# Decode attention with a GeGLU gate: one stream of 2 MB cache loads with 16 KB rows in place of 256 KB loads with 2 KB rows

## The chip, the cores and the metric

The kernel runs on one core of one Trainium2 chip. The metric is device microseconds of one execution. Before the change it takes 151.41 us (median of 4 runs, 151.3 to 152.01). A run counts as slow when it is over 1.5% above the fastest of the same kernel; a single run of a kernel has no known state. The span of a profile is about 1.9 us shorter than the time, because it runs from the first to the last instruction. In the views, PE is the matrix engine, DVE and ACT are the vector and scalar engines, SP is the engine whose queue issues the loads, and SBUF is the on-chip memory that the loads fill, 128 partitions of it here. A packet is one record of the DMA trace; for these loads it is one row.

## The reference, cut to what matters

```python
xn = layernorm(x)                                  # x: 8 x 1 x 512
q  = (xn @ wq)                                     # 32 query heads of 128
k, v = k_cache[:, :, 3072:, :], v_cache[...]       # 8 batches, 8 kv heads, last 1024 of 4096 tokens
s  = softmax(q k^T / sqrt(128)) v @ wo             # 4 query heads share a kv head
g  = silu((gelu(xn @ w_gate) * (xn @ w_up)) @ w_down)
out = x + s * g
```

The window of one (batch, kv head) pair is 256 KB without a gap; the next head's window begins 1 MB further on. All inputs are bf16: 33.6 MB of K and V windows (8 batches, K and V, 2 MB each) and 13.9 MB of weights, 47.5 MB together. The loads set the floor: at the 416 GB/s of the weight stretch below, 47.5 MB would take 114 us (an estimate from that stretch) of the 149.5.

## The kernel before

```python
    for hkv in range(Hkv):                       # K stage
        for b in range(B):
            k_sb = k_pool.tile([P, NSC, Dh], BF16, name="k_sb")          # 6 buffers
            nc.sync.dma_start(out=k_sb,
                in_=A_k_cache[b, hkv, win0:Sk, :].rearrange("(p c) d -> p c d", c=NSC))
            ...8 transposes -> kT_ps; copy to kT; 8 score matmuls, 4 wide; exp -> pT_all
    ...softmax sums for all pairs                # [cut]
    for hkv in range(Hkv):                       # V stage
        for b in range(B):
            ...load v_sb the same way; 8 value matmuls; oT_all = oT_ps * 1/sum
        nc.sync.dma_start(out=wo_sb[:, hkv*rep:(hkv+1)*rep, :], in_=...)   # 1 KB rows
        ...4 matmuls of 512 columns into s_ps
```

One load is one head's window: 128 partitions, 8 tokens each, so 128 rows of 2 KB. Source and destination both have one outer dimension of 128. wq, the FFN weights and the FFN come first, then all of K, then all of V with wo in eight pieces.

The softmax here doesn't subtract the row's maximum and nothing guards it: scores larger than these inputs give would overflow.

Of the kernel before, what the change touches and what calls it, by code (L numbers as in the profile page):

```python
# [7 lines left out]
ACT = mybir.ActivationFunctionType  # L9
# [3 lines left out]
FP32 = mybir.dt.float32  # L13


@with_exitstack
def kernel(
# [22 lines left out]
    NDC = D // 128  # L40
    NFC = F // 128
    NSC = W // 128
    inv_sqrt_dh = float(Dh) ** -0.5

    P = nc.NUM_PARTITIONS
    NG = Hkv * B
    GB = 16

    consts = ctx.enter_context(tc.tile_pool(name="consts", bufs=1))
    weights = ctx.enter_context(tc.tile_pool(name="weights", bufs=1))  # L50
    persist = ctx.enter_context(tc.tile_pool(name="persist", bufs=1))
    ffn_sb = ctx.enter_context(tc.tile_pool(name="ffn_sb", bufs=1))
    k_pool = ctx.enter_context(tc.tile_pool(name="k_pool", bufs=6))
    kT_pool = ctx.enter_context(tc.tile_pool(name="kT_pool", bufs=4))
    v_pool = ctx.enter_context(tc.tile_pool(name="v_pool", bufs=20))
    small = ctx.enter_context(tc.tile_pool(name="small", bufs=3))
# [4 lines left out]
        out=ident,  # L61
        in_=ident,
        compare_op=ALU.not_equal,
        fill=1.0,
        base=0,
        pattern=[[-1, P]],
        channel_multiplier=1,
    )
    ones_pp = consts.tile([P, P], BF16, name="ones_pp")
    nc.vector.memset(ones_pp, 1.0)  # L70

    x_flat = A_x.flatten_outer_dims()
    x_sb = persist.tile([B, D], BF16, name="x_sb")
    nc.sync.dma_start(out=x_sb, in_=x_flat)

    wq_sb = weights.tile([P, NDC, Hq * Dh], BF16, name="wq_sb")
    nc.sync.dma_start(out=wq_sb, in_=A_wq.rearrange("(k p) n -> p k n", p=P))
    wg_sb = weights.tile([P, NDC, F], BF16, name="wg_sb")
    nc.scalar.dma_start(out=wg_sb, in_=B_w_gate.rearrange("(k p) n -> p k n", p=P))
    wu_sb = weights.tile([P, NDC, F], BF16, name="wu_sb")  # L80
    nc.gpsimd.dma_start(out=wu_sb, in_=B_w_up.rearrange("(k p) n -> p k n", p=P))
    wd_sb = weights.tile([P, NFC, D], BF16, name="wd_sb")
    nc.scalar.dma_start(out=wd_sb, in_=B_w_down.rearrange("(k p) n -> p k n", p=P))
    wo_sb = weights.tile([P, Hq, D], BF16, name="wo_sb")

    eps_sb = consts.tile([B, 1], FP32, name="eps_sb")
    nc.vector.memset(eps_sb, 1e-5)

    stats = persist.tile([B, nc.vector.BN_STATS_DIM], FP32, name="stats")
    nc.vector.bn_stats(out=stats, in_=x_sb)  # L90
    mv = persist.tile([B, nc.vector.BN_AGGR_DIM], FP32, name="mv")
    nc.vector.bn_aggr(out=mv, in_=stats)
    rstd = persist.tile([B, 1], FP32, name="rstd")
    nc.scalar.activation(
        out=rstd, in_=mv[:, 1:2], func=ACT.Sqrt, bias=eps_sb, scale=1.0
    )
    nc.vector.reciprocal(out=rstd, in_=rstd)
    xhat = persist.tile([B, D], BF16, name="xhat")
    nc.vector.tensor_scalar(  # L99
        out=xhat,  # L100
        in0=x_sb,
        scalar1=mv[:, 0:1],
        scalar2=rstd[:, 0:1],
        op0=ALU.subtract,
        op1=ALU.mult,
    )

    xnT_sb = persist.tile([P, NDC, B], BF16, name="xnT_sb")
    qT_all = persist.tile([P, B, Hq], BF16, name="qT_all")
    oT_all = persist.tile([P, Hq, B], BF16, name="oT_all")  # L110
    hT_sb = persist.tile([P, NFC, B], BF16, name="hT_sb")
    g_sb = persist.tile([B, D], FP32, name="g_sb")
    pT_all = persist.tile([P, NG, NSC, rep], BF16, name="pT_all")
    sums_sb = persist.tile([P, NG, rep], FP32, name="sums_sb")
    recip_all = persist.tile([P, NG, rep], FP32, name="recip_all")

    with tc.tile_pool(name="ps_xnT", bufs=1, space=bass.MemoryType.PSUM) as ps_xnT_pool:
        xnT_ps = ps_xnT_pool.tile([P, NDC, B], BF16, name="xnT_ps")
        for k in range(NDC):
            nc.tensor.transpose(  # L120
                xnT_ps[:, k, :],
                xhat[:, k * 128 : (k + 1) * 128],
                ident[0:B, 0:B],
            )
        nc.vector.tensor_copy(out=xnT_sb, in_=xnT_ps)

    HB = 8
    qctx = ExitStack()
    ps_q = qctx.enter_context(tc.tile_pool(name="ps_q", bufs=2, space=bass.MemoryType.PSUM))
    for m0 in range(0, Hq, HB):  # L130
        qT_ps = ps_q.tile([P, HB, B], FP32, name="qT_ps")
        for mi in range(HB):
            m = m0 + mi
            for k in range(NDC):
                nc.tensor.matmul(  # L135
                    qT_ps[:, mi, :],
                    wq_sb[:, k, m * Dh : (m + 1) * Dh],
                    xnT_sb[:, k, :],
                    start=(k == 0),
                    stop=(k == NDC - 1),  # L140
                )
        nc.vector.tensor_copy(  # L142
            out=qT_all[:, :, m0 : m0 + HB],
            in_=qT_ps.rearrange("p h b -> p b h"),
        )

    fctx = ExitStack()
    ffn_ps = fctx.enter_context(tc.tile_pool(name="ffn_ps", bufs=1, space=bass.MemoryType.PSUM))
    gu_ps = ffn_ps.tile([P, NFC, 2, B], FP32, name="gu_ps")
    for j in range(NFC):  # L150
        for w, wsb in enumerate((wg_sb, wu_sb)):
            for k in range(NDC):
                nc.tensor.matmul(  # L153
                    gu_ps[:, j, w, :],
                    wsb[:, k, j * 128 : (j + 1) * 128],
                    xnT_sb[:, k, :],
                    start=(k == 0),
                    stop=(k == NDC - 1),
                )
    zT = gu_ps[:, :, 0, :]  # L160
    uT = gu_ps[:, :, 1, :]
    z2 = ffn_sb.tile([P, NFC, B], FP32, name="z2")
# [4 lines left out]
    u3 = ffn_sb.tile([P, NFC, B], FP32, name="u3")  # L167
    nc.vector.tensor_tensor(out=u3, in0=z2, in1=zT, op=ALU.mult)
    th = ffn_sb.tile([P, NFC, B], FP32, name="th")
    nc.scalar.activation(out=th, in_=u3, func=ACT.Tanh, scale=0.7978845608028654)  # L170
    gm = ffn_sb.tile([P, NFC, B], FP32, name="gm")
    nc.vector.tensor_scalar(
        out=gm, in0=th, scalar1=0.5, scalar2=0.5, op0=ALU.mult, op1=ALU.add
    )
    gz = ffn_sb.tile([P, NFC, B], FP32, name="gz")
    nc.vector.tensor_tensor(out=gz, in0=gm, in1=zT, op=ALU.mult)
    nc.vector.tensor_tensor(out=hT_sb, in0=gz, in1=uT, op=ALU.mult)

    f_ps = ffn_ps.tile([B, D], FP32, name="f_ps")
    for j in range(NFC):  # L180
        nc.tensor.matmul(  # L181
            f_ps,
            hT_sb[:, j, :],
            wd_sb[:, j, :],
            start=(j == 0),
            stop=(j == NFC - 1),
        )
    th2 = ffn_sb.tile([B, D], FP32, name="th2")
    nc.scalar.activation(out=th2, in_=f_ps, func=ACT.Tanh, scale=0.5)
    nc.vector.tensor_scalar(  # L190
# [4 lines left out]
    p1ctx = ExitStack()  # L195
    ps_kT = p1ctx.enter_context(tc.tile_pool(name="ps_kT", bufs=2, space=bass.MemoryType.PSUM))
    ps_sc = p1ctx.enter_context(tc.tile_pool(name="ps_sc", bufs=2, space=bass.MemoryType.PSUM))

    gi = 0
    for hkv in range(Hkv):  # L200
        for b in range(B):
            k_sb = k_pool.tile([P, NSC, Dh], BF16, name="k_sb")
            nc.sync.dma_start(
                out=k_sb,
                in_=A_k_cache[b, hkv, win0:Sk, :].rearrange(
                    "(p c) d -> p c d", c=NSC
                ),
            )
            kT_ps = ps_kT.tile([P, W], BF16, name="kT_ps")
            for c in range(NSC):  # L210
                nc.tensor.transpose(  # L211
                    kT_ps[:, c * 128 : (c + 1) * 128],
                    k_sb[:, c, :],
                    ident,
                )
            kT = kT_pool.tile([P, W], BF16, name="kT")
            nc.vector.tensor_copy(out=kT, in_=kT_ps)  # L217
            sc_ps = ps_sc.tile([P, NSC, rep], FP32, name="sc_ps")
            qg = qT_all[:, b, hkv * rep : (hkv + 1) * rep]
            for c in range(NSC):  # L220
                nc.tensor.matmul(  # L221
                    sc_ps[:, c, :],
                    kT[:, c * 128 : (c + 1) * 128],
                    qg,
                    start=True,
                    stop=True,
                )
            nc.scalar.activation(  # L228
                out=pT_all[:, gi, :, :],
                in_=sc_ps,  # L230
                func=ACT.Exp,
                scale=inv_sqrt_dh,
            )
            gi += 1
# [108 lines left out]
```

## Time and profile before

| | before |
|---|---|
| time | 151.4 us |
| span of the profile | 149.5 us |
| bytes moved, mean rate | 47.74 MB, 319 GB/s |
| wq and FFN weights, 4 to 22 us | 416 GB/s |
| K stage, 40 to 86 us | 304 GB/s, PE busy 40.3 of 46 us |
| V stage with wo, 88 to 142 us | 365 GB/s |

From the page of the kernel before, part 2: the span in 40 slices, in tenths; DMA is the busy share of the 16 DMA engines, GB/s what they moved.

```profile
PEclk9999999999999999689999999755555555555555
DMA  4999999957999699889989899999999999999900
GB/s 117 430 419 416 407 403 372 372 161 212 315 390 368 211 342 325 252 278 298 298 321 323 263 311 309 393 372 378 372 380 371 376 357 380 337 386 380 349 30 2
DMA packets 25843, 47.74 MB, mean 319 GB/s; under 512 B 2256, under 2 KB 8160, under 8 KB 25312
```

From the view by stretches of the kernel before; the last three columns are granted TensorE clock, DMA share and GB/s.

```profile
4.00:22.00 18.00, 2.16 (x63) 1.90 (x63) 0.53 (x2) 0.00 (x0) 0.00 (x0) 1.00 1.02 416
40.00:86.00 46.00, 40.27 (x817) 35.04 (x815) 36.94 (x56) 10.18 (x52) 0.00 (x0) 0.96 0.90 304
88.00:142.00 54.00, 35.70 (x605) 22.17 (x602) 16.31 (x69) 1.14 (x6) 0.00 (x0) 0.57 1.03 365
```

The chain of waits of the kernel before, part 4 of the page:

```profile
DMA 66%; PE 24%; DVE 5%; issue 3%; SPq 1%
```

Two lines of the view of what its load queue waited for (us in total, times, longest):

```profile
SPq L203 <- PE sc_ps L221: 21.0, 31, 1.0
...
SPq L203 <- PE kT_ps L211: 7.7, 19, 1.3
```

Read together: in the K stage the DMA engines are not always busy (0.90) and the queue waits for PE to give K buffers back. In the V stage they are always busy (1.03), yet move 365 GB/s where the weight stretch moved 416. So there are two things to win: PE work spread over more traffic, and longer rows.

### The profile page before, as it was taken

What the parts mean: (1) busy time and instruction counts of PE and PEld (TensorE: products, weight loads), DVE (VectorE), ACT (ScalarE), POOL (GpSimd) and SP (SyncE); (2) the same over time, 40 slices, a digit from 0 to 9 for tenths busy, and PEclk for the clock granted to TensorE, in tenths of its full rate; (3) what the DMA queues carried; (4) which work ended last, traced back from release to release, by engine and by line L of the source; (5) the groups of instructions that cost most, each with busy time, mean ns of one, the idle gap of its engine ahead of it and who ended that gap; (6) DMA issues with size and microseconds to landing.
All of it is one profiled execution on the core that took longest, in us unless ns stands there. A gap on an engine that the chain in (4) does not pass through costs nothing.

```text
span 149.5 us, 4236 instructions
## 1 busy us (share of the span) xinstructions
PE 97.0 (65%) x1830; PEld 73.4 (49%) x1830; DVE 64.2 (43%) x154; ACT 16.5 (11%) x70; POOL 1.4 (1%) x6
## 2 busy tenths in 40 slices
PE   0000137499988896998998996597474748585760
PEld 0000127497466785987876874453433334342420
DVE  2100001057296885788788885831211121121213
ACT  4000000052122221222222221000000000000000
POOL 3000000000000000000000000000000000000000
PEclk9999999999999999689999999755555555555555
DMA  4999999957999699889989899999999999999900
GB/s 117 430 419 416 407 403 372 372 161 212 315 390 368 211 342 325 252 278 298 298 321 323 263 311 309 393 372 378 372 380 371 376 357 380 337 386 380 349 30 2
DMA packets 25843, 47.74 MB, mean 319 GB/s; under 512 B 2256, under 2 KB 8160, under 8 KB 25312
## 3 DMA queue, kind: packets, MB, share of 16 engines
q1 hardware_dynamic: 23216, 41.97, 79.9%
q10 hardware_dynamic: 2336, 3.67, 7.1%
q0 software_dynamic: 272, 1.84, 2.9%
q8 instruction: 14, 0.23, 0.6%
q14 instruction: 5, 0.04, 0.1%
HBM read 47.46 MB, written 0.01 MB: 318 GB/s over the span
## 4 chain that ended last, share of the span: by engine, by line
DMA 66%; PE 24%; DVE 5%; issue 3%; SPq 1%
DMA v_sb<-in_A_v_cache_dram 22%; DMA k_sb<-in_A_k_cache_dram 17%; DMA wq_sb<-in_A_wq_dram 15%; DMA wo_sb<-in_A_wo_dram 12%; PE kT_ps L211 10%; PE s_ps L300 4%; PE sc_ps L221 4%; DVE kT L217 3%; PE qT_ps L135 2%; PE f_ps L181 2%; PE gu_ps L153 1%; SPq L269 1%; DVE tmp L309 0%; DVE out_sb L311 0%; SPq L292 0%
## 5 line engine op out<-in xcount | busy, mean ns | idle before, releaser
L217 DVE COPY kT<-kT_ps 128x1024 bf16<-128x1024 bf16 x64 | 43.6, 690 | 14.4 <-PE kT_ps L211 14.1
L211 PE MATMUL kT_ps<-ident,k_sb 128*128 128x128 bf16 x512 | 41.6, 228 | 3.2 <-DMA k_sb<-in_A_k_cache_dram 3.2
L211 PEld LDWEIGHTS <-k_sb 128*128 128x128 bf16 x512 | 31.3, 102 | 3.8 <-DMA k_sb<-in_A_k_cache_dram 3.8
L284 DVE TENSOR_TENSOR oT_all<-oT_ps,recip_all 128x4 bf16<-128x4 f32 x64 | 11.0, 175 | 36.4 <-PE oT_ps L277 35.4
L277 PE MATMUL oT_ps<-pT_all,v_sb 128*128 128x4 bf16 x512 | 19.9, 167 | 10.2 <-DMA v_sb<-in_A_v_cache_dram 7.3
L277 PEld LDWEIGHTS <-v_sb 128*128 128x128 bf16 x512 | 16.8, 105 | 19.4 <-DMA v_sb<-in_A_v_cache_dram 10.6
L221 PE MATMUL sc_ps<-qT_all,kT 128*128 128x4 bf16 x512 | 22.7, 166 | 3.8 <-DVE kT L217 1.7
L221 PEld LDWEIGHTS <-kT 128*128 128x128 bf16 x512 | 17.9, 97 | 10.0 <-DVE kT L217 8.5
L300 PE MATMUL s_ps<-wo_sb,oT_all 128*8 128x512 bf16 x32 | 14.9, 620 | 8.0 <-DMA wo_sb<-in_A_wo_dram 8.0
L228 ACT ACTIVATE pT_all<-sc_ps 128x32 bf16<-128x32 f32 x64 | 12.6, 197 | 43.9 <-PE sc_ps L221 43.9
L153 PE MATMUL gu_ps<-xnT_sb,wg_sb 128*128 128x8 bf16 x56 | 3.4, 168 | 12.5 <-DMA wg_sb<-in_B_w_gate_dram 10.4
L142 DVE CAST qT_all<-qT_ps 128x64 bf16<-128x64 f32 x4 | 0.9, 225 | 21.3 <-PE qT_ps L135 21.3
L300 PEld LDWEIGHTS <-oT_all 128*8 128x8 bf16 x32 | 3.3, 106 | 12.8 <-issue 10.3
L153 PEld LDWEIGHTS <-wg_sb 128*128 128x128 bf16 x56 | 2.7, 104 | 10.5 <-DMA wg_sb<-in_B_w_gate_dram 10.5
L135 PE MATMUL qT_ps<-xnT_sb,wq_sb 128*128 128x8 bf16 x128 | 3.6, 168 | 3.4 <-DMA wq_sb<-in_A_wq_dram 3.4
L135 PEld LDWEIGHTS <-wq_sb 128*128 128x128 bf16 x128 | 3.5, 104 | 3.5 <-DMA wq_sb<-in_A_wq_dram 3.5
L153 PEld LDWEIGHTS <-wu_sb 128*128 128x128 bf16 x56 | 2.6, 104 | 5.2 <-DMA wu_sb<-in_B_w_up_dram 3.0
L153 PE MATMUL gu_ps<-xnT_sb,wu_sb 128*128 128x8 bf16 x56 | 3.1, 168 | 2.9 <-DMA wu_sb<-in_B_w_up_dram 2.9
L163 ACT ACTIVATE z_381<-gu_ps 128x112 f32<-128x112 f32 x1 | 0.3, 264 | 26.8 <-PE gu_ps L153 26.8
L252 DVE TENSOR_REDUCE sums_sb<-sums_ps 128x64 f32<-128x512 f32 x4 | 2.7, 684 | 1.1 <-PE sums_ps L243 1.1
L181 PE MATMUL f_ps<-wd_sb,hT_sb 128*8 128x512 bf16 x14 | 3.2, 379 | 0.0
L120 PE MATMUL xnT_ps<-ident,xhat 8*128 8x8 bf16 x4 | 0.3, 168 | 4.4 <-DVE xhat L99 4.4
(33 smaller groups left out, 15.9 us busy)
## 6 DMA issues: line engine op xcount, KB each, us to landing
k_sb<-in_A_k_cache_dram SPq DMA_DIRECT2D x64, 256.0 KB, 4.3
v_sb<-in_A_v_cache_dram SPq DMA_DIRECT2D x64, 256.0 KB, 6.1
wq_sb<-in_A_wq_dram SPq DMA_DIRECT2D x1, 4096.0 KB, 22.0
wo_sb<-in_A_wo_dram SPq DMA_DIRECT2D x8, 512.0 KB, 6.2
wg_sb<-in_B_w_gate_dram ACTq DMA_DIRECT2D x1, 1792.0 KB, 14.3
wd_sb<-in_B_w_down_dram ACTq DMA_DIRECT2D x1, 1792.0 KB, 32.1
wu_sb<-in_B_w_up_dram POOLq DMA_DIRECT2D x1, 1792.0 KB, 16.9
x_sb<-in_A_x_dram SPq DMA_DIRECT2D x1, 8.0 KB
```

The source lines that it names most:

```text
L135: nc.tensor.matmul(qT_ps[:, mi, :], wq_sb[:, k, m * Dh : (m + 1) * Dh], xnT_sb[:, k, :], start=(k == 0), stop=(k == NDC - 1),)
L153: nc.tensor.matmul(gu_ps[:, j, w, :], wsb[:, k, j * 128 : (j + 1) * 128], xnT_sb[:, k, :], start=(k == 0), stop=(k == NDC - 1),)
L181: nc.tensor.matmul(f_ps, hT_sb[:, j, :], wd_sb[:, j, :], start=(j == 0), stop=(j == NFC - 1),)
L211: nc.tensor.transpose(kT_ps[:, c * 128 : (c + 1) * 128], k_sb[:, c, :], ident,)
L217: nc.vector.tensor_copy(out=kT, in_=kT_ps)
L221: nc.tensor.matmul(sc_ps[:, c, :], kT[:, c * 128 : (c + 1) * 128], qg, start=True, stop=True,)
L228: nc.scalar.activation(out=pT_all[:, gi, :, :], in_=sc_ps, func=ACT.Exp, scale=inv_sqrt_dh,)
L252: nc.vector.tensor_reduce(out=sums_sb[:, i * GB : (i + 1) * GB, :], in_=sums_ps.rearrange("p (g c j) -> p g j c", g=GB, c=NSC, j=rep), axi ...
L269: nc.sync.dma_start(out=v_sb, in_=A_v_cache[b, hkv, win0:Sk, :].rearrange("(p c) d -> p c d", c=NSC),)
L277: nc.tensor.matmul(oT_ps, v_sb[:, c, :], pT_all[:, gi, c, :], start=(c == 0), stop=(c == NSC - 1),)
L284: nc.vector.tensor_tensor(out=oT_all[:, hkv * rep : (hkv + 1) * rep, b], in0=oT_ps, in1=recip_all[:, gi, :], op=ALU.mult,)
L300: nc.tensor.matmul(s_ps, oT_all[:, h, :], wo_sb[:, h, :], start=(h == 0), stop=(h == Hq - 1),)
```

## The change

Its intent is one unbroken stream of large loads. A ring of ten 16 KB-per-partition slots takes all big loads in order. A slot holds a whole batch of K or V: eight heads, each on 16 partitions of 64 tokens, so a row is 16 KB. A chunk of 128 partitions then mixes eight heads, so scores are computed 32 wide for all query heads and a mask, added by a matmul with the identity, removes the wrong heads before the exponential. K and V of consecutive batches alternate; weights of the FFN and wo come last; the attention output is rearranged on chip to match 16 KB rows of wo.

```diff
-            nc.sync.dma_start(out=k_sb, in_=A_k_cache[b, hkv, win0:Sk, :].rearrange("(p c) d -> p c d", c=NSC))
+    def load_cache(cache, b, name):
+        t = ring.tile([P, NCH, Dh], BF16, name=name, tag="slot")        # ring: 10 slots
+        nc.sync.dma_start(
+            out=t.rearrange("p c d -> p (c d)"),
+            in_=cache[b, :, win0:Sk, :].rearrange("n (p c) d -> p n (c d)", p=PS),   # PS = 16
+        )
+    def load_rows(src, rows, r0, n, name): ...   # weights: [128, 16 KB] from "(p r) n -> p r n"
+    def scores(b, g):
+        nc.tensor.matmul(sc_ps, ident, mask, start=True, stop=False)     # 512 wide, new
+        for c in range(GC): nc.tensor.matmul(sc_ps[:, c, :], kT chunk, qT[:, b, :], ...)   # 32 wide
+    def values(b): ...4 sum matmuls of 512, 64 value matmuls 32 wide
+    for b in range(B):
+        k_t[b] = load_cache(A_k_cache, b, "k_t"); v_t[b-1] = load_cache(A_v_cache, b-1, "v_t")
+        ...transposes(b), scores(b), values(b-1) interleaved, in emission order
+    ...w_gate, w_up, last V, w_down, wo (last piece: 4 rows); FFN; output rows matched on chip
```

The destination of a cache load is 128 partitions. Its source is 16 token slices (16 KB apart) by 8 heads (1 MB apart), and it is given in that order.

## The prediction

> **What bounds the kernel now.** The execution moves 47.74 MB in a 149.5 us span (mean 319 GB/s, queue table); no engine is busy more than 65% of it. Two stages lose against the best rate that the same page shows. From 4 to 22 us, when wq (8 KB rows) and the FFN weights stream, the stretch-by-stretch view gives 401 to 432 GB/s. From 40 to 86 us (K stage) it gives only 270 to 350: each 256 KB tile runs transpose, copy, score in turn, PE is busy 84 to 94% of these stretches, and about 0.84 us per tile is about 310 GB/s; with 6 K buffers, the queue's own waits are for the score matmuls (21.0 us) and the transposes (7.7 us). From 88 to 142 us (V stage) the DMA share is full, yet only 371 to 387 GB/s arrive, with 2 KB rows for V and 1 KB rows for wo. The chain of waits is 66% DMA, 24% PE.
>
> **What changes.** Bytes stay (47.45 MB of inputs). All large loads become one SP stream of about 2 MB transfers with rows of mostly 16 KB; K and V are interleaved, so PE work of a batch (scores and values) spreads over 4 MB of traffic, and ten slots let loads run about 40 us ahead. I estimate 415 to 430 GB/s throughout: the trace's 8 KB-row stretch, slightly bettered.[...]
>
> **PE after, warm costs from the timeline view.** A transpose pair takes 60 ns (8 in 0.48 us), a weight load with a narrow matmul 27 ns (128 pairs in 3.5 us), a 512-wide matmul 223 ns (14 in 3.1 us). Per batch: 64 transposes 3.8 + 64 scores 1.7 + 4 masks 0.9 + 4 sums 0.9 + 64 values 1.7 = 9.0 us, against 4.19 MB / 422 GB/s = 9.9 us of DMA. Masks and sums are new cost (about 7 us each in total), but PE has just enough room: 90% loaded while warm. DVE needs 8 copies of 0.69 plus about 1 us, 6.5 us per batch; ACT, four 512-wide exponentials at an estimated 0.6, 2.4 us. Neither binds.
>
> **Critical path after.** First bytes about 2.6 us (as now), 47.45 MB at 422 GB/s = 112.4, so the last wo rows land near 115. The last V lands near 101; its values, the on-chip row matching (two 2048-wide DVE products, estimated 1 to 2 us each, 32 narrow matmuls) take about 10 us and hide under wd and wo. After the last 512 KB: 16 narrow matmuls about 0.6, two 128-wide DVE ops about 0.5 (now 1.4), output DMA and end 2.5 as now. Span about 119; time runs 1.9 above the span: **121.5 us, range 118 to 128**. Chances: faster by over 2% 0.93, same 0.03, slower 0.04.
>
> **What shows each step.** DMA share full from 3 to 115 us at 415+ GB/s; no hole where SP waits for a slot; PE 85 to 95% busy with clock near 1.0 in the middle; chain of waits mostly DMA, ending in wo; less than 5 us from last landing to end.
>
> **What would make it wrong.** (1) PE slower than 9.9 us per batch (bubbles at the mask, three transpose banks, or the clock dropping to 0.5 as it does in the V stage now): backlog fills the slots and moves the end, up to some 10 us. (2) The 16-by-8-row source[...]: rate well under 400 GB/s. (3) Uneven DMA engines at the end.

(The rate of 422 GB/s is the estimate from the stretch of 401 to 432, and the sum stands: 2.6 + 112.4 + 0.6 + 0.5 + 2.5 = 118.6 us of span, given there as about 119; the 1.9 us from span to time make it 120.5.)

## More of the kernel before

The comparison with the reference is lenient here: it also passed the four experiments that read wrong cache rows on purpose (e1, e2, e5, e6). So passing says little about the cache path; the mapping of each right version was checked by reading.

## The result, and the profile after

The changed kernel takes 200.57 us (median of 4, 198.97 to 203.41; the slowest of them counts as slow). The ratio to the kernel before is 1.325 (95% interval 1.310 to 1.341). Ratios here are the mean time of the fast runs over that of the fast runs of the kernel before in the same rounds, so not quite the ratio of the medians. The prediction of 121.5 us was wrong in direction and by 79 us.

The same part of the page, after:

```profile
PEclk9999999696759685995798596859755896555555
DMA  6999999999999999999999999999999999999950
GB/s 224 423 358 212 209 212 212 209 216 209 216 216 216 212 211 216 229 242 219 245 229 252 216 229 226 226 219 226 229 222 219 231 413 295 219 234 410 423 240 6
DMA packets 3561, 47.74 MB, mean 242 GB/s; under 512 B 464, under 2 KB 472, under 8 KB 600
```

The stretches, after: wq; the caches, in two lines; w_gate and w_up; the last V; w_down and wo.

```profile
4.00:12.00 8.00, 0.51 (x6) 0.34 (x6) 2.02 (x10) 1.10 (x1) 0.00 (x0) 1.00 1.01 429
20.00:100.00 80.00, 48.91 (x813) 42.34 (x818) 29.86 (x48) 10.75 (x18) 0.00 (x0) 0.81 1.01 219
100.00:150.00 50.00, 26.69 (x502) 23.25 (x505) 15.81 (x27) 5.38 (x9) 0.00 (x0) 0.74 1.01 227
160.00:165.00 5.00, 4.91 (x116) 4.57 (x113) 1.59 (x3) 1.20 (x2) 0.00 (x0) 0.98 1.06 406
166.00:174.00 8.00, 4.35 (x70) 4.24 (x70) 0.02 (x1) 0.26 (x1) 0.00 (x0) 0.50 1.01 222
180.00:187.00 7.00, 3.79 (x119) 3.34 (x116) 4.38 (x9) 0.28 (x1) 0.00 (x0) 0.50 1.01 425
```

The chain of waits after:

```profile
PE 45%; another core or an unknown queue 29%; DMA 21%; SPq 1%; issue 1%; DVE 0%
```

What the load queue waited for after, the longest line:

```profile
SPq L96 <- DMA k_t<-in_A_k_cache_dram: 46.3, 5, 10.2
```

From the view of all waits after, what PE waited for in its transposes of K and in its value matmuls:

```profile
PE kT_ps L190 <- DMA k_t<-in_A_k_cache_dram: 43.4, 8, 7.2
PE oT_ps L224 <- DMA v_t<-in_A_v_cache_dram: 18.5, 8, 3.5
```

Three readings. First, the DMA share is full all the time, so nothing holds the loads up; what the queue waits for is earlier loads, not PE giving slots back. Second, the weight stretches run at 406 to 429 GB/s and the cache stretches at 219 to 227, even a single V load between two weights (166 to 174 us). Third, a packet of 16 KB takes 0.61 us in wq and 1.24 us in the caches (30 to 60 us; worked out from the trace's packet records). The share shows only that engines are occupied; the rate shows that each row takes twice as long. The chain of waits alone would mislead: it credits PE with 45%, yet PE waits 43.4 us for K and 18.5 us for V in total.

At the mean of 222 GB/s over 20 to 150 us, 33.55 MB of caches take 151 us; at the 424 GB/s that a later run reached they take 79. The difference of 72 us is nearly all of the distance to that run's span (197.5 against 121.7 us).

### The profile page after: what moved, and what is told of

Same layout as the page of the kernel before. It is cut to its first block, busy times and chain, and to the rows that moved or that the text cites. A ratio compares the mean times of both kernels' runs of the same rounds, so it can differ in the third digit from the quotient of the medians.

```text
span 197.5 us, 4405 instructions
## 1 busy us (share of the span) xinstructions
PE 107.9 (55%) x2053; PEld 93.7 (47%) x2062; DVE 63.2 (32%) x120; ACT 22.8 (12%) x38; POOL 1.4 (1%) x6
## 4 chain that ended last, share of the span: by engine, by line
PE 45%; another core or an unknown queue 29%; DMA 21%; SPq 1%; issue 1%; DVE 0%
DMA v_t<-in_A_v_cache_dram 21%; PE kT_ps L190 18%; PE oT_ps L224 7%; PE sc_ps L206 5%; PE sc_ps L201 4%; PE gu_ps L272 4%; PE sum_ps L218 3%; PE s_ps L348 2%; PE f_ps L319 1%; SPq L96 1%; PE r_ps L329 0%; SPq L91 0%; PE o_ps L303 0%; DVE oT L232 0%
## 5 line engine op out<-in xcount | busy, mean ns | idle before, releaser
L190 PE MATMUL kT_ps<-ident,k_t 128*128 128x128 bf16 x512 | 48.7, 272 | 43.4 <-DMA k_t<-in_A_k_cache_dram 43.4
L190 PEld LDWEIGHTS <-k_t 128*128 128x128 bf16 x512 | 42.2, 125 | 44.2 <-DMA k_t<-in_A_k_cache_dram 44.2
L210 ACT ACTIVATE pT<-sc_ps 128x512 bf16<-128x512 f32 x32 | 19.1, 597 | 139.5 <-PE sc_ps L206 139.4
L224 PE MATMUL oT_ps<-pT,v_t 128*128 128x32 bf16 x512 | 14.4, 179 | 18.5 <-DMA v_t<-in_A_v_cache_dram 18.5
L224 PEld LDWEIGHTS <-v_t 128*128 128x128 bf16 x512 | 13.6, 98 | 22.9 <-DMA v_t<-in_A_v_cache_dram 22.9
L206 PE MATMUL sc_ps<-qT,kT 128*128 128x32 bf16 x512 | 18.9, 182 | 0.2 <-issue 0.2
L201 PE MATMUL sc_ps<-mask,ident 128*128 128x512 bf16 x31 | 15.8, 510 | 0.0
L218 PE MATMUL sum_ps<-pT,ones_pp 128*128 128x512 bf16 x24 | 7.1, 410 | 0.7 <-issue 0.2
L228 DVE TENSOR_REDUCE sums<-sum_ps 128x32 f32<-128x512 f32 x8 | 5.5, 688 | 4.5 <-PE sum_ps L218 4.5
L201 PEld LDWEIGHTS <-ident 128*128 128x128 bf16 x32 | 4.1, 127 | 0.0
```

Source lines behind the costliest of these rows:

```text
L190: nc.tensor.transpose(kT_ps[:, i * P : (i + 1) * P], k_t[b][:, g * GC + t * TG + i, :], ident)
L201: nc.tensor.matmul(sc_ps.rearrange("p c h -> p (c h)"), ident, mask.rearrange("p c n j -> p (c n j)"), start=True, stop=False, skip_group_ ...
L206: nc.tensor.matmul(sc_ps[:, c, :], kTs[b, g, c // TG][:, (c % TG) * P : (c % TG + 1) * P], qT[:, b, :], start=False, stop=(c == GC - 1), s ...
L210: nc.scalar.activation(out=pT[b][:, g * GC : (g + 1) * GC, :], in_=sc_ps, func=ACT.Exp, scale=inv_sqrt_dh)
L218: nc.tensor.matmul(sum_ps.rearrange("p c h -> p (c h)"), ones_pp, pT[b][:, g * GC : (g + 1) * GC, :].rearrange("p c h -> p (c h)"), start= ...
L224: nc.tensor.matmul(oT_ps, v_t[b][:, c, :], pT[b][:, c, :], start=(c == 0), stop=(c == NCH - 1))
```

## The experiments

Eighteen experiments ran, and all passed the comparison with the reference, with the caveat above. Many are single runs, whose state is unknown. The differences in time read from them are mostly tens of us; four runs of one experiment spread by at most 14 us (e3), then 9.5 us (e16). In the cut diffs, `flat` is the K or V cache seen as rows of 16 KB in e1 and e2, and wq seen so elsewhere. These theories were set against each other:

- **P, partitions written together.** How long a row takes depends on which partitions are written at the same time, and the 16-by-8 load writes rows together that slow each other, where a load with one outer dimension of 128 does not. "In step" means that such rows are written at the same time, and a lead or step of some engines over others is to keep them apart. Which rows of a cache load are written together no trace here shows: a packet record has queue, kind, start, duration and size, but neither engine nor partition.
- **H, memory.** Rows 1 MB apart slow the reading.
- **S, shape.** A source of two outer dimensions is slow as such, wherever its rows land.

Packet means below are of 16 KB packets in the stretch from 30 to 60 us, unless another is named, from the trace's records. Where the expectations speak of engines, of steps and of drifting, they speak as theory P has it, not from a trace.

### e1: the same shape, rows close together

```diff
-            in_=cache[b, :, win0:Sk, :].rearrange("n (p c) d -> p n (c d)", p=PS),
+            in_=flat[b*512 : b*512+144].rearrange("(p m) x -> p m x", m=9)[:, 0:8, :],   # wrong result on purpose
```

> The changed kernel, but each cache load reads 16 groups of 8 neighbouring 16 KB rows (one row of gap between groups) instead of rows 1 MB apart; same 16-by-8 source shape, same destination; wrong result on purpose. Theory P[...]: the cache stretches stay near 212 GB/s, a 16 KB packet near 1.25 us, time near 200 us. Theory H[...]: above 400 GB/s, packet near 0.61 us, time 120 to 128 us.

Measured: 198.12 us (one run), packets 1.23 us. From the view by stretches of e1:

```profile
20.00:100.00 80.00, 47.95 (x813) 41.54 (x818) 30.39 (x49) 10.75 (x18) 0.00 (x0) 0.81 1.01 223
```

Theory H falls as the cause: with rows 16 KB apart the loads are just as slow.

### e2: rows far apart, one dimension of 128

```diff
+            in_=flat.rearrange("(q s) x -> q s x", s=32)[:, 4 * b, :],    # 128 rows, 512 KB pitch; wrong result on purpose
```

> The changed kernel, but each cache load reads 128 rows of 16 KB at a single pitch of 512 KB, so that source and destination both have one dimension of 128; wrong result on purpose. Theory P:[...] above 400 GB/s, time 120 to 128 us. Theory H: slow as before or slower, at most 250 GB/s, time 190 us or more.

Measured: 123.49 us (one run), packets 0.62 us. From the view by stretches of e2:

```profile
20.00:80.00 60.00, 55.23 (x1194) 49.02 (x1199) 41.01 (x68) 15.50 (x26) 0.00 (x0) 0.97 1.01 424
80.00:110.00 30.00, 25.37 (x584) 22.48 (x584) 15.22 (x31) 4.45 (x10) 0.00 (x0) 0.86 1.00 422
```

Same bytes, same rows of 16 KB, same destination tile: twice the rate. A pitch of 512 KB costs nothing here. This run is also what the prediction described, 2 us from its 121.5. Everything in the change but the shape of the cache load works.

### e5 and e6: e2's source, cut by destination

```diff
+        for q in range(0, P, 64):       # e6: 16
+            nc.sync.dma_start(out=t[q : q + 64], in_=rows[q : q + 64])     # rows: e2's source
```

> The fast run e2 (128 cache rows at one pitch of 512 KB, wrong result on purpose) with each cache load cut by destination into partitions 0-63 and 64-127, each with one dimension of 64 on both sides. Theory P[...]: about 212 GB/s, 16 KB packets 1.25 us, time 195 to 205 us. Rival S (the two-dimensional source shape itself is what slows, not where rows land): still above 400 GB/s, packets 0.61 us, time 121 to 126 us.

> As e5, but cut into 8 loads of 16 neighbouring partitions[...]. Theory P:[...] packets 2.2 to 2.5 us, cache stretches near 107 GB/s, time 330 to 370 us[...]. Rival S: above 380 GB/s, time 121 to 132 us.

Measured: e5 206.01 us and 1.25 us a packet; e6 272.44 us and 2.03 us a packet (one run each). From the views by stretches of e5, then of e6:

```profile
20.00:100.00 80.00, 46.81 (x797) 41.30 (x798) 28.47 (x46) 10.15 (x17) 0.00 (x0) 0.81 1.01 212
```

```profile
20.00:100.00 80.00, 30.02 (x503) 26.34 (x504) 18.43 (x30) 5.97 (x10) 0.00 (x0) 0.72 1.01 130
100.00:180.00 80.00, 32.67 (x520) 27.81 (x518) 19.04 (x31) 7.16 (x12) 0.00 (x0) 0.67 1.02 151
```

Theory S falls: these loads have one outer dimension on both sides and read the rows that e2 read at 424 GB/s. Cutting the destination in two halves the rate. Smaller loads by themselves do not explain it: the kernel before moved 365 GB/s in its V stage with loads of 256 KB, each to 128 partitions. e6 was expected to be slower still (330 to 370 us); its packets begin at 2.07 us and shorten with time (1.7 us after 120 us); why was not shown.

### e9: sets of partitions by themselves

```diff
+    for g, (k, p0, step) in enumerate(groups):          # ahead of the 2 KB-row version e4
+        n = NCH * Dh - 128 * (g + 1)                    # row length marks the group
+        for t in probes:                                # 4 loads
+            nc.sync.dma_start(out=t[p0 : p0+(k-1)*step+1 : step, 0:n], in_=flat[0:k, 0:n])
```

> The 2 KB-row version e4 with 60 small loads ahead of it, 15 groups of 4 loads with one row of 14 to 16 KB for each of 2, 4, 8 or 16 partitions (each group has its own row length, so its packets can be told in the trace); right result, time means nothing. Theory P, in us for a row scaled to 16 KB[...]: partitions 0,4: 0.61; 0,32: 1.25; 0,1: 1.25; 0,64: 0.61; 8,16: 0.61; 0-3: 2.0-2.5; 0,32,64,96: 1.25; 0,16,32,48: 1.25; 0,4..28: 0.61; 0-7: 2.0-2.5; 0,16..112: 1.25; 0,8..120: 1.25; 0-15: 2.0-2.5; 0,4..60: 1.25; 64,68..92: 0.61.[...]

Measured, us for a row scaled to 16 KB, median (lowest to highest), from the packet records. The row length of the 0,16,32,48 group is also that of the FFN weights, but its 16 packets start between 33 and 37 us and the weights' after 160 us. Each load has one row for each partition named:

```
partitions         rows in a load   median (lowest to highest)
0, 4                     2          0.61 (0.61 to 0.92)
8, 16                    2          0.61 (0.61 to 0.61)
64, 68 .. 92             8          0.63 (0.61 to 1.48)
0, 4 .. 28               8          0.83 (0.61 to 1.07)
0, 64                    2          0.87 (0.61 to 1.17)
0, 32                    2          1.21 (0.61 to 1.29)
0, 1                     2          1.29 (1.28 to 1.29)
0, 32, 64, 96            4          1.16 (0.61 to 1.30)
0, 16, 32, 48            4          1.06 (0.61 to 1.65)
0, 16 .. 112             8          1.24 (0.82 to 2.27)
0, 8 .. 120             16          1.06 (0.75 to 1.72)
0, 4 .. 60              16          1.29 (0.87 to 2.35)
0, 1, 2, 3               4          1.87 (0.81 to 2.55)
0 .. 7                   8          2.40 (0.96 to 2.45)
0 .. 15                 16          2.42 (0.95 to 2.46)
```

Ends of neighbouring groups overlap, which widens the ranges. The loads of a group size read the same source rows, so the partitions written make the difference, and not their number alone. Two rows to 0 and 4 or to 8 and 16 took 0.61 us each, the time of a row of wq, and eight to 64, 68 .. 92 took 0.63. Two rows to 0 and 32 took 1.21 and two to 0 and 1 took 1.29; four neighbours took 1.87, and eight or sixteen 2.40 and 2.42. That is the first half of P: some partitions, written together, double or quadruple the time of a row. Six groups lie outside what was expected: 0.83 (0, 4 .. 28) and 0.87 (0, 64) where 0.61 was said, 1.06 twice and 1.16 where 1.25 was said, 1.87 where 2.0 to 2.5 was said; that stays unexplained.

### e3, e7, e8: engines put out of step through the wq load

If rows slow each other only when they are written at the same time, a lead of half a load for some of the engines should cure it with the cache loads untouched. That cutting the wq load gives such a lead was the assumption; no trace shows it.

```diff
-    wq_t = [load_rows(A_wq, KD, k, 2, "wq_t") for k in (0, 2)]
+    for k, cuts in ...:                  # e3: 96,12,12,4,4 partitions in both halves of wq
+        for p0, p1 in cuts:              # e7: 112,12,4 in one half; e8: in both
+            nc.sync.dma_start(out=t[p0:p1], in_=w[p0:p1])
```

> The changed kernel with its cache loads untouched and a right result; only the wq load is cut by partitions (96, 12, 12, 4, 4 of each half)[...]. Theory P[...]:[...] cache stretches near 420 GB/s, packets near 0.61 us, time 121 to 128 us[...]. Theory H: cache stretches stay near 212 GB/s, time 198 to 204 us.

> The changed kernel, cache loads untouched, right result; the second wq load is cut into partitions 0-111, 112-123 and 124-127. In e3 such 12-partition loads took 2.2 us a row[...]. Theory P: cache stretches start at 350 to 420 GB/s and packets near 0.65 us; if the step is kept, time 123 to 135 us; if it drifts, 140 to 185 us. Rival S: 212 GB/s, time 199 to 205 us.

> As e7, but both wq loads are cut so[...]. Theory P:[...] cache stretches start at 215 to 260 GB/s; slower than e7[...]. A theory in which any disorder helps: as fast as e7 or faster. Rival S: 212 GB/s throughout.

Measured: e3 188.25 us in its one fast run (188.25 to 202.29 in four); its profile is of the slowest run, 202.29 us, with 269 GB/s from 40 to 80 us and 242 from 80 to 120; e7 204.19 us, ratio 1.335 (1.320 to 1.349), 222 GB/s from 20 to 100 us; e8 209.78 us, ratio 1.375 (1.353 to 1.396), 222 GB/s from 30 to 100 us. Only e3 helped, and only partly. In the form in which it was put, "a lead is enough", the theory failed three times. The doses were badly made, too: the small loads were slow themselves (some packets took 2.2 to 2.6 us), so the lead was probably not the intended one. These runs neither support P nor refute it.

### e10, e11, e12: one load per head, halves alternating

```diff
+        for n in range(Hkv):
+            q = 64 * (n % 2) + n // 2
+            nc.sync.dma_start(out=t[q : q + 61 : 4], in_=cache[b, n, win0:Sk, :].rearrange("(p c) d -> p (c d)", p=PS))
+    # e11, e12: 1 or 2 loads of 8 rows to partitions 0, 4 .. 28, ahead of everything
```

> The changed kernel with one load per head, its 256 KB as 16 rows of 16 KB to partitions 4 apart in one half (0-63 for even heads, 64-127 for odd ones), mask to match, right result. Theory P:[...] in step, about 212 GB/s and 1.25 us a packet, time 195 to 210 us.[...] If engines drift on their own: 230 to 300 GB/s.

> As e10, with one load of 8 rows (partitions 0, 4 .. 28[...]) ahead of everything[...]. Halves alternate row by row, so under theory P with the step kept[...]: 400 to 425 GB/s, 0.61 us a packet, 122 to 130 us. If the step is lost as in e7: 212 to 260 GB/s, 170 to 205 us.[...]

> As e11 with two such loads[...]. Theory P with the step kept: as slow as e10. Any disorder helps: as fast as e11.

Measured: e10 181.48 us (one run), e11 181.70 us (ratio 1.203, 1.189 to 1.218), e12 167.83 us (one run); packets 1.06, 1.07 and 0.95 us. Already e10 was faster than P in step says (195 to 210 us, 1.25 us a packet); its 246 GB/s from 20 to 100 us lie in the 230 to 300 expected if engines drift, but no drift was shown. One step did nothing and two helped (in a single run), the reverse of what P with a kept step says. The timeline of e15 below suggests why the dose cannot be trusted.

### e13: GpSimd's queue

```diff
-        nc.sync.dma_start(          # in load_cache
+        nc.gpsimd.dma_start(
```

> The changed kernel with the cache loads issued from GpSimd's queue instead of SyncE's, all else untouched, right result. If that queue[...]: above 390 GB/s in the cache stretches, 122 to 135 us. If it deals as SyncE's does (theory P unchanged): 205 to 250 GB/s, 180 to 205 us. I expect the second, 65 to 35.

Measured: 227.61 us (one run), 222 GB/s from 20 to 100 us, packets 1.24 us. The other queue does not cure it (that it would was the first case of the expectation). The whole is 27 us slower than the changed kernel, outside the range expected. The page of e13 shows a likely part: from 6 to 203 us its slices stand at 203 to 264 GB/s, weights included, while the changed kernel's weights ran at 406 to 429. At about 230 instead of 420 GB/s, 13.9 MB of weights take 27 us more (an estimate from these rates; no run tested it).

### e14, e15, e16, e18: two halves, and a lead that is really made

```diff
+        for h in range(2):              # e14: heads 0-3 to partitions 0-63, 4-7 to 64-127; mask to match
+            nc.sync.dma_start(out=t[64*h : 64*h+64], in_=cache[b, 4*h:4*h+4, win0:Sk, :].rearrange("n (p c) d -> p n (c d)", p=PS))
+    # e15: 4 loads of 8 rows to partitions 0, 4 .. 28, ahead of everything
+    # e16, e18: 4 or 2 of them to partitions 64, 68 .. 92, between wq and the first cache load
```

> The changed kernel with two loads per cache slot, heads 0-3 to partitions 0-63 and heads 4-7 to 64-127, mask to match, right result.[...] Theory P, in step: 205 to 235 GB/s, 1.2 to 1.3 us a row, 190 to 207 us.

> As e14, with 4 loads of 8 rows[...] ahead of everything[...]. Theory P with the step kept: 400 to 425 GB/s, 0.61 us a row, 123 to 131 us. If[...] the step is lost where weights and cache loads meet: like e14, or between (140 to 190 us).

Measured: e14 203.09 us (one run), packets 1.24 us, as P says. From the view by stretches of e14:

```profile
20.00:100.00 80.00, 46.49 (x807) 40.96 (x808) 28.77 (x47) 10.16 (x17) 0.00 (x0) 0.79 1.01 213
```

e15 201.57 and 203.47 us in its fast runs; packets 1.19 us in its profile, which is of a slow run (204.72 us): no cure. The queue's timeline of e15 (start, duration, what) suggests why:

```profile
0.73 2.86 SPq L106 DMA_DIRECT2D step<-in_A_wq_dram  x4
3.63 0.91 SPq L91 DMA_DIRECT2D wq_t<-in_A_wq_dram  x2
```

Issuing the four step loads took 2.86 us, longer than the 2.4 us of lead they were to make (4 rows of 0.61). So there was probably nothing queued to run ahead with; that is inferred. The same may hold for e11 and e12, where the step loads also went first. So e16 issues them after wq (wq at 0.73 us, the step loads from 1.64), when there is work queued, and to partitions 64, 68 .. 92:

> As e15, but the 4 step loads are issued after wq and write partitions 64, 68 .. 92[...]. Theory P, and engines keep the step they have (nothing pulls them together): 400 to 425 GB/s and 0.61 to 0.65 us a row in the cache stretches, 123 to 131 us. If[...]: 210 to 260 GB/s, 185 to 206 us.

> As e16 with 2 step loads: 2 of 4 rows overlap, so at first a mean of (2 x 0.61 + 2 x 1.29) / 4 = 0.95 us a row, about 275 GB/s; if the step is kept, 155 to 170 us. If pulled into step: as e14, 203 us. If pushed apart: as e16.

Measured: e16 164.37 and 165.89 us in its fast runs, ratio 1.110 (1.092 to 1.128); e18 198.96 us (one run). So e16 lies between its two cases, a lead that is kept and one that is lost. From the view by stretches, e16 first, then e18:

```profile
12.00:16.00 4.00, 2.65 (x99) 2.65 (x100) 0.00 (x0) 0.00 (x0) 0.00 (x0) 1.00 1.01 393
16.00:32.00 16.00, 11.66 (x226) 11.07 (x225) 8.42 (x14) 2.92 (x5) 0.00 (x0) 1.00 1.02 382
32.00:44.00 12.00, 7.45 (x161) 6.20 (x159) 5.23 (x9) 1.40 (x4) 0.00 (x0) 0.92 1.02 320
44.00:56.00 12.00, 7.79 (x165) 6.64 (x163) 5.30 (x9) 2.26 (x4) 0.00 (x0) 0.93 1.01 278
104.00:116.00 12.00, 8.20 (x119) 7.33 (x117) 4.87 (x8) 1.79 (x3) 0.00 (x0) 0.73 1.02 235
```

```profile
16.00:34.00 18.00, 9.99 (x181) 9.28 (x180) 7.06 (x11) 1.79 (x3) 0.00 (x0) 0.97 1.00 262
36.00:100.00 64.00, 37.59 (x679) 32.33 (x682) 22.96 (x38) 8.36 (x14) 0.00 (x0) 0.78 1.01 221
```

Now the dose and the rate agree. In the first 16 us of a stretch of caches (16 to 32 us) a row takes 1.24 us with no lead (e14), 1.01 with two step loads (e18; 0.95 was expected, an estimate from the 0.61 and 1.29 of e9 that assumes two rows of four to be written together) and 0.69 with four (e16). Same loads, same bytes, same destinations: only the step loads ahead of them differ. So the time of a row is not fixed by its load; it depends on what went before. That what is written together changed with it is P's reading, and this is the strongest evidence for it. The gain then wears off, in e18 by 36 us (221 GB/s from there to 100 us), in e16 unevenly until 104 us (235 GB/s from there to 116 us).

### e17: whole loads with a lead

```diff
+    for p0, k in ((0, 12), (64, 4)):     # between wq and the first cache load
+        nc.sync.dma_start(out=step[p0 : p0 + k], in_=flat[0:k])
```

> The changed kernel, cache loads whole and untouched, right result, with two small loads between wq and the first cache load: 12 rows of 16 KB to partitions 0-11[...] and 4 rows to partitions 64-67[...].[...] Theory P: 350 to 425 GB/s in the first cache loads. If the in-flight limit wears the step off, it holds longer than in e16: 125 to 160 us. If[...] the limit does not matter: 160 to 200 us.

Measured: 200.91 us, ratio 1.336 (1.329 to 1.343); 226 GB/s from 20 to 30 us, while packets between 12 and 16 us took 0.86 to 3.22 us (median 2.11). The start missed the 350 to 425 GB/s expected. Whether any lead came of the step loads was not shown. Whether the limit on loads in flight (see the end of the point-by-point section) wears a lead off stays open.

### e4: one dimension of 128, with 2 KB rows

```diff
-            in_=cache[b, :, win0:Sk, :].rearrange("n (p c) d -> p n (c d)", p=PS),
+            out=t.rearrange("p (n c) d -> p n (c d)", n=Hkv),
+            in_=cache[b, :, win0:Sk, :].rearrange("n (p c) d -> p n (c d)", p=P),     # 128 slices x 8 heads
```

Each chunk of 128 partitions now belongs to one head, so the mask matmuls go, scores and values are 4 wide, and the sums take one matmul a batch. The rest of the change stays.

> The changed kernel with 2 KB rows: one 2 MB load per batch still, but 128 token slices by 8 heads, so its first dimension is 128; each chunk then belongs to one head, and the mask matmuls go, scores and values are 4 wide. Right result. Theory P: cache stretches at 370 to 390 GB/s as in the V stage of the kernel before, time 127 to 134 us. Theory H predicts the same[...]. This tells whether the rest of the change (order, ring, wo last) works once the loads run.

Measured: 131.39 us (131.31 to 131.45), ratio to the kernel before 0.873 (0.869 to 0.877). From the view by stretches of e4:

```profile
4.00:12.00 8.00, 0.50 (x6) 0.34 (x6) 1.57 (x8) 1.10 (x1) 0.00 (x0) 1.00 1.00 427
20.00:90.00 70.00, 58.34 (x1251) 57.57 (x1250) 42.16 (x73) 5.80 (x26) 0.00 (x0) 0.76 1.04 385
```

This is the version to keep: 13% faster than the kernel before and 69 us faster than the change as made. The caches at 385 GB/s instead of e2's 424 cost 33.55 MB/385 - 33.55 MB/424 = 8.0 us, and e4 is 7.9 us slower than e2.

## Why the prediction was wrong, point by point

- **What bounds the kernel before.** Right as far as tested: e4 gains 19 us (150.63 to 131.39, medians of the same chip) with V's row length unchanged. Its DMA share is full over the caches (1.04 at 385 GB/s, where the K stage before had 0.90 at 304), although its load queue still waits for PE to give slots back, 49 us in total.
- **"I estimate 415 to 430 GB/s throughout: the trace's 8 KB-row stretch, slightly bettered."** This is the step that failed. It held for the weights (406 to 429) and failed for the caches (219 to 227), which are 71% of the bytes. I costed a load by its row length alone and carried the rate of loads with one outer dimension of 128 over to loads with 16 by 8. Row length gains what was said (2 KB rows 385, 16 KB rows 424 in e2); the shape lost a factor of two.
- **The warning was there, and underweighted.** Point (2) of what would make it wrong names the 16-by-8 source and "rate well under 400 GB/s", yet slower got a chance of 0.04. The dimensions of both sides stood in the diff; nothing in the trace of before could tell their cost, so the honest range was far wider.
- **PE work.** Right in total, as e2 shows: 55.23 of 60 us busy (92%; 90% was said), clock 0.97, DMA never held up. About 7 us each was said for sums and masks. The masks took 12.0 us; the sums 7.1 us for the 24 of 32 that were recorded, so about 9.5 for all (an estimate).
- **Exponentials and row matching.** Estimated 0.6 us and 1 to 2 us; e2 has 0.597 and 1.22 to 1.23.
- **The end.** In e2 the last wo rows land at 116.2 us (near 115 was said), but 64 matmuls follow for 1.9 us instead of 16 for 0.6, and the end comes 5.5 us after the landing, not 3.6. So the span is 121.7 us where the terms said give 118.6.
- **"SP waiting for no slot, DMA share full."** Both came true in the slow kernel as well. As tests they were too weak: they cannot tell fast rows from slow ones. Only the rate could.

What is shown: memory pitch (e1, e2), source shape as such (e5) and row length are not the cause; the time of a row depends on which partitions are written together (e9: 0.61 us for 0 and 4, 1.21 for 0 and 32, 1.29 for 0 and 1, with the six exceptions named), and on the same loads it changes with the small loads ahead of them (e14 1.24 us, e18 1.01, e16 0.69). What is argued, and was not shown: that the changed kernel's cache loads write rows together that slow each other, since the trace names neither engine nor partition of a packet. What stays open: why the gain of e16 wears off. In the changed kernel's queue the twelfth and thirteenth big loads leave at 34.35 and 44.29 us, just when PE's waits for the fourth and fifth end (34.34 and 44.28 us). So a load seems to be issued only when the load eight before has landed; whether that is what wears it off, e17 failed to tell.

## What to carry to other kernels

Give a large load one outer dimension of 128 on both sides, even at the price of shorter rows: here 2 KB rows with 128 outside (385 GB/s, e4) beat 16 KB rows with 16 by 8 (219). When the DMA share is full, compare GB/s and the time of one packet between loads of the same row length before believing that the loads are at their limit. Small loads ahead of the large ones were no cure here: four of them brought 382 GB/s from 16 to 32 us (e16, against e14's 213 over 20 to 100 us), but it did not last.
